# Dilated attention and gated unit: eight transfer semaphores in the scheduler's model, the v block moved to partitions 16 to 127, w_out exchanged on TensorE

## The chip, the cores and the metric

The kernel runs on one core of a Trainium2 chip. The time is that of one execution on the device in microseconds (us), taken as the median of several runs. The core has a matmul engine (TensorE, PE in the profile), a vector engine (VectorE, DVE), an engine for activations and copies (ScalarE, ACT), GpSimd (POOL), and a queue from which transfers are issued in order (SyncE, SP). The transfers themselves run on 16 transfer engines. On-chip data lies in 128 partitions of SBUF[...].

## The reference: what is computed

```python
# q, k, v: (8, 8, 576, 64)  batch, heads, positions, head size; float32
scores = q @ k.transpose(0, 1, 3, 2) / 8
rel = pos[:, None] - pos[None, :]
mask_plain = (rel >= 0) & (rel < 32)                       # heads 0 to 3
mask_dil = (rel >= 0) & (rel < 128) & (rel % 4 == 0)       # heads 4 to 7
attn = softmax(where(mask, scores, -1e9)) @ v
x = attn.transpose(0, 2, 1, 3).reshape(8, 576, 512)
# gated unit, per batch
gate = sigmoid(causal_conv(x, conv_w))                     # 5 taps, per channel
out = (gate * (x @ w_val)) @ w_out                         # (8, 576, 512) float32
```

A batch is handled as two units of four heads: one dilated, one plain. In a dilated unit the positions are sorted by their remainder modulo 4, so that the dilated window becomes a plain band of 32 in each of the four sets of 144 positions.

## The kernel before

The kernel is fully unrolled. Every piece of work is a task with the engines it may run on, its cost there, what it depends on, and a key. A greedy scheduler, at build time, runs through a model of the engines, takes again and again the task that can start first (among those that can start about then, the one with the lowest key), and emits all instructions in the order of the modelled start times. Each engine executes its own instructions in that order. So the keys and the modelled costs change the order of the work, and in part the engine, but not what is computed.

```python
KEY = {"L": 2.5, "cv": -28.5, "T": -2.0, "ET": -28.0, "S": -10.2, "X": -30.2, "M": -1.7,
       "A": -17.7, "N": -14.4, "XT": 3.7, "XE": -24.0, "C": 1.1, "H": -26.4, "V": 4.1,
       "G": -9.6, "O": 12.5, "P": -23.7, "SP": 2, "W": 5.4, "WV": 1, "WO": 2}
# L loads, T transposes of q and k, ET their eviction, S scores, X exp, M mask, A attention,
# N division, XT transposes of x, XE their eviction, C conv, H tanh, V x @ w_val, G gate,
# O output product, P its eviction; W: penalty for a change of TensorE's configuration;
# WV, WO: the unit behind whose loads w_val and w_out are loaded
...
    def start_of(self, t, eng):
        s = self.free_at[eng]
        if eng == "PE" and t.cfg != self.cfg and self.cfg is not None:
            s += self.SWITCH
        for d in t.deps:
            s = max(s, d.fin + self.LAT)
        if t.after:                      # a load does not start before the load ahead of it
            s = max(s, t.after.start)
        ...
        return max(s, self.slot_for(t)[0])
...
    # in commit(): a transfer in the model
        if t.load:
            self.dma = max(self.dma, s + 1.4) + t.load
            t.fin = self.dma + 0.6
...
    def fill(self, a, b):                # matmuls on a zero tile where TensorE would be idle (line 604)
        ...
```

The tasks of the loads, with the modelled transfer time as the last number, and the layout of the dilated v. `rows` is v as (positions of a set, head, 4 x 64 values): the first block has the positions 0 to 79 of each set, the second the positions 32 to 143, both from partition 0 on.

```python
    KB = (80, 112)
    T1 = TT - KB[1]          # TT = 144
...
    def load_vd(u, n, z):
        b = units[u][0]
        rows = v[b, 4:8].rearrange("h (p r) d -> p h (r d)", r=R)
        nc.sync.dma_start(out=vas[z][n % 2], in_=rows[z * T1:z * T1 + KB[z]])
...
            L[u] = dma(f"ld{name}{u}", j0 + KEY["L"], 1.8, ...)               # q or k: 576 KB
            ldv[u] = [dma(f"vd{z}{u}", j0 + KEY["L"], (1.0, 1.4)[z], ...)     # dilated v: 320, 448 KB
            ldv[u] = [dma(f"vp{u}{h}", j0 + KEY["L"], 1.4, ...)               # plain v: 384 KB, twice
...
        if u == KEY['WV']:
            load_w("val", moe_w_val, w_val[0], 0)      # two loads of 512 KB, casts to bf16
            exchanged_val()
        if u == KEY['WO']:
            load_w("out", moe_w_out, w_out[0], 6)
            exchanged_out()
```

The conv leaves its result for the second half of the positions with the two halves of the partitions exchanged. So a second copy of w_out is needed, with its rows exchanged in the same way; it is made by two transfers from SBUF to SBUF (line 644):

```python
    def exchanged_out():
        for h in range(2):
            W_OX.append(dma(f"out_x{h}", 11, 0.9, lambda h=h: nc.sync.dma_start(
                out=w_out[1][64 * h:64 * h + 64], in_=w_out[0][64 - 64 * h:128 - 64 * h]),
                W_OK["out"]))
```

The lines that the prediction speaks of: 370 and 373 load q and k (dilated and plain), 380 the dilated v, 388 and 392 the plain v, 591 issues the stores, 604 is the idle fill, 447 the exp, 427 the scores, 561 the product with w_val, 577 the one with w_out, 582 its eviction, 281 and 279 are the copies and casts through a helper.

Of the kernel before, what the change touches and what calls it, by code (L numbers as in the profile page):

```python
# [13 lines left out]
def hi_bf16(ap: bass.AP) -> bass.AP:  # L14
# [2 lines left out]
    return b[idx]  # L17


KEY = {"L": 2.5, "cv": -28.5, "T": -2.0, "ET": -28.0, "S": -10.2, "X": -30.2, "M": -1.7,  # L20
       "A": -17.7, "N": -14.4, "XT": 3.7, "XE": -24.0, "C": 1.1, "H": -26.4, "V": 4.1,
       "G": -9.6, "O": 12.5, "P": -23.7, "SP": 2, "W": 5.4, "WV": 1, "WO": 2}


class Task:
# [16 lines left out]
class Plan:  # L42


    LAT = 0.09
    SWITCH = 0.095
    BIAS = {"DVE": 0.4, "POOL": -0.8}
    GAP = 0.35
# [3 lines left out]
    def __init__(self, pairs, score_pairs):  # L52
        self.tasks = []
        self.free_at = {e: 0.0 for e in self.SLACK}
        self.banks = [0.0] * (2 * pairs)
        self.score_pairs = score_pairs
        self.scores = []
        self.cfg = None
        self.dma = 0.0
        self.port = {"DVE": 0.0, "POOL": 0.0}  # L60
        self.idle = None
        self.done = []
# [22 lines left out]
# [6 lines that stand above are left out]
        if t.after:  # L91
            s = max(s, t.after.start)
        if eng in t.port:
            s = max(s, self.port["POOL" if eng == "DVE" else "DVE"])
        return max(s, self.slot_for(t)[0])

    def fits(self, t, eng):
        if len(t.opts) == 1:
# [4 lines left out]
    def commit(self, t, eng, s):  # L103
        inf = float("inf")
        occ, lat = t.opts[eng]
        before = self.free_at[eng]
        self.free_at[eng] = s + occ
        t.fin = s + lat
        if t.load:
            self.dma = max(self.dma, s + 1.4) + t.load  # L110
            t.fin = self.dma + 0.6
        if eng in t.port:
            self.port[eng] = s + lat
        if eng == "PE":
            self.cfg = t.cfg
            self.fill(before, s)
        if t.need:
            t.slot = self.slot_for(t)[1]
            for n in t.slot:
                self.banks[n] = inf  # L120
            if t.need == "score":
                self.scores.append(inf)
                t.order = len(self.scores) - 1
            t.last = 0.0
        for f in t.frees:
            f.holders -= 1
            f.last = max(f.last, t.fin + self.LAT)
            if f.holders == 0:
                for n in f.slot:
                    self.banks[n] = f.last  # L130
                if f.need == "score":
                    self.scores[f.order] = f.last
        t.start, t.eng = s, eng
        self.done.append(t)
# [52 lines left out]
def kernel(  # L187
# [17 lines left out]
    W = 32  # L205
    TT = S // R
    QB = TT // 2
    KB = (80, 112)
    T1 = TT - KB[1]
    JP, JD = 9, 18  # L210
    scale = 1.0 / float(D) ** 0.5
    NCH = Dm // 128
# [36 lines left out]
    gy = consts.tile([128, NCH, 2, B, HALF], BF16, name="gy")  # L249

    ident_b = consts.tile([128, 128], BF16, name="ident_b")
    ident_2 = consts.tile([128, D], BF16, name="ident_2")
    ident_f = consts.tile([8, 8], FP32, name="ident_f")
    mask_d = consts.tile([128, HALF], BF16, name="mask_d")
# [42 lines left out]
    def const(name, eng, dur, emit, deps=(), key=-50):  # L297
        return plan.add(name, key, {eng: (dur, dur + 0.05)}, lambda t: emit(), deps,
                        port=("POOL",))

    c_warm = const("warm0", "DVE", 0.5, lambda: nc.vector.memset(warm, 0.0), key=-60)  # L301
    c_eye = const("eye", "POOL", 1.0, lambda: eye(ident_b, 128), key=-60)

    def dil_mask():
        nc.gpsimd.memset(mask_d, 1.0)
        for z in range(2):
            band(mask_d[:, 2 * QB * z:2 * QB * (z + 1)].rearrange("p (h t) -> p h t", h=2),
                 z * (QB - T1), [[0, 2], [1, QB]], 1)

# [27 lines left out]
    def dve_consts():  # L337
        for x in kTs:
            nc.vector.memset(x[:, 0:W], 0.0)
            nc.vector.memset(x[:, W + 2 * S:], 0.0)  # L340
        for x in ets:
            nc.vector.memset(x[:, :, HALF:], 1.0)
        nc.vector.memset(xT[:, :, :, 0:K - 1], 0.0)
        nc.vector.memset(vps[0][0:W // 2, 0], 0.0)
    c_dv = const("dve_consts", "DVE", 2.2, dve_consts, key=-59)


# [29 lines left out]
    def load_vd(u, n, z):  # L377
        b = units[u][0]
        rows = v[b, 4:8].rearrange("h (p r) d -> p h (r d)", r=R)
        nc.sync.dma_start(out=vas[z][n % 2], in_=rows[z * T1:z * T1 + KB[z]])  # L380

    def load_vp(u, n, half):
        b = units[u][0]
# [235 lines left out]
    def load_w(name, src, dst, key):  # L619
        parts = []  # L620
        for half in range(2):
            deps = [W_OK["val"][2 * half], W_OK["val"][2 * half + 1]] if name == "out" else []
            ld = dma(f"w_{name}{half}", key, 1.7, lambda half=half: nc.sync.dma_start(  # L623
                out=wst[half],
                in_=src.rearrange("(c p) n -> p c n", p=128)[:, 2 * half:2 * half + 2]), deps, lane=lane)
            for c in range(2):
                parts.append(add(
                    f"cast_{name}{half}{c}", key + 2, {"ACT": (0.52, 0.62), "DVE": (0.35, 0.42)},
                    lambda t, half=half, c=c: copy(t, dst[:, 2 * half + c], wst[half][:, c]),
                    [ld], port=("DVE",)))  # L630
        W_OK[name] = parts
# [9 lines left out]

    def exchanged_out():
        for h in range(2):
            W_OX.append(dma(f"out_x{h}", 11, 0.9, lambda h=h: nc.sync.dma_start(
                out=w_out[1][64 * h:64 * h + 64], in_=w_out[0][64 - 64 * h:128 - 64 * h]),
                W_OK["out"]))

    ldq, ldk, ldv, cvq, cvk = {}, {}, {}, {}, {}
    Tq, Tk, Eq, Ek = {}, {}, {}, {}
# [6 lines left out]
    for u in range(NU):  # L656
# [4 lines left out]
        for name, L, TQ in (("q", ldq, Tq), ("k", ldk, Tk)):  # L661
            dep = []
            if u >= NQ:
                p = u - NQ
                if units[p][1]:
                    dep = [TQ[p]]
                else:
                    dep = [(cvq if name == "q" else cvk)[p]]
            L[u] = dma(f"ld{name}{u}", j0 + KEY["L"], 1.8, lambda u=u, name=name: load_q(u, name), dep, lane=lane)
        if d:  # L670
            dep = [cvv[(same[-2], e, z)] for e in range(2) for z in range(2)] if len(same) > 1 else []
            ldv[u] = [dma(f"vd{z}{u}", j0 + KEY["L"], (1.0, 1.4)[z],
                          lambda u=u, n=len(same), z=z: load_vd(u, n, z), dep, lane=lane)
                      for z in range(2)]
        else:
            dep = [cvp[2 * same[-2] + e] for e in range(2)] if len(same) > 1 else [c_dv]
            ldv[u] = [dma(f"vp{u}{h}", j0 + KEY["L"], 1.4,
                          lambda u=u, n=len(same), h=h: load_vp(u, n, h), dep, lane=lane)
                      for h in range(2)]
            for name, C, L, TQ, cs in (("k", cvk, ldk, Tk, kcs), ("q", cvq, ldq, Tq, qcs)):  # L680
                dep = [TQ[same[-2]]] if len(same) > 1 else []
                C[u] = add(f"cv{name}{u}", j0 + KEY["cv"], {"POOL": (1.10, 1.16), "ACT": (1.05, 1.15)},
                           lambda t, u=u, name=name: copy(
                               t, (qcs if name == "q" else kcs)[(u // 2) % 2].rearrange(
                                   "p j h d -> p h j d"),
                               (qns if name == "q" else kns)[u % NQ].rearrange(
                                   "p (h j d) -> p h j d", h=2, j=JP)),
                           [L[u]] + dep, port=("POOL",))
# [120 lines left out]
    for n in range(NF):  # L809
        for f in range(2):  # L810
            z = len(ST)
            b0, b1 = 128 * n // HALF, (128 * n + 127) // HALF
            key = 8 * b1 + 7 + KEY["O"] + (z % 4)
            ou = add(f"O{f}{n}", key, {"PE": (0.86, 1.03)}, lambda t, f=f, n=n: outs(t, f, n),
                     [GA[(b, c)] for b in range(b0, b1 + 1) for c in range(NCH)]
                     + (W_OX if f else W_OK["out"]), cfg="F", need="bank")
            cp = add(f"P{f}{n}", 8 * b1 + 7 + KEY["P"], {"ACT": (0.52, 0.60), "DVE": (0.60, 0.68)},
                     lambda t, ou=ou, f=f, n=n, z=z: out_copy(t, ou, f, n, z),
                     [ou] + ([ST[z - NO]] if z >= NO else []), frees=[ou])
            ST.append(dma(f"st{f}{n}", key - 20, 0.7, lambda f=f, n=n, z=z: store(f, n, z), [cp]))  # L820

    plan.run()

# [29 lines left out]
```

## Time and profile before

| | |
|---|---|
| time, median of 3 runs | 202.44 us (201.51 to 207.02) |
| span of the profiled execution | 200.5 us |
| TensorE busy, matmuls | 168.8 us (84%), 2887 of them |
| VectorE busy | 122.1 us (61%) |
| ScalarE busy | 122.7 us (61%) |
| GpSimd busy | 60.0 us (30%) |
| transferred | 43.94 MB, of them 33.56 MB read from memory and 9.44 MB written to it |
| packets of the main queue | 81.2% of the 16 engines' span |
| granted TensorE clock, mean | 0.961 of full speed |

The busy times are for the whole span and don't say when an engine is the limit; the slices, the stages and the issue queue, which the prediction shows, do. TensorE's busy time includes the idle fill: 14.3 us in 51 matmuls (line 604), all of it in the first 50 us. The exchange of w_out shows as two transfers of 256 KB with 10.7 us from issue to landing.

### The profile page before, as it was taken

The numbers are of one execution on the slowest core, as the hardware profiler recorded it, in microseconds if no ns is written. First come the engines' busy times: TensorE is split into PE (matmuls) and PEld (weight loads), VectorE is DVE, ScalarE is ACT, GpSimd is POOL, SyncE is SP. The second block draws the span as 40 slices with busy tenths as digits, with TensorE's granted clock in tenths as the row PEclk, the third lists the DMA queues.
The fourth block names the chain that finished last, engine by engine and source line by source line (L and its number), as shares of the span: only waits on it lengthen the run. The fifth ranks groups of instructions, "written<-read, shape, count | busy, mean of one in ns | idle before, by whom it ended". The sixth has DMA issues, their size and how long they took to land.

```text
span 200.5 us, 6725 instructions
## 1 busy us (share of the span) xinstructions
PE 168.8 (84%) x2887; PEld 115.0 (57%) x2887; DVE 122.1 (61%) x233; ACT 122.7 (61%) x205; POOL 60.0 (30%) x98
## 2 busy tenths in 40 slices
PE   7987799695999788769889697999899979989890
PEld 2544476473576646646466474767567767557640
DVE  4393759575377767437656483776767877861600
ACT  2555857572884848812878357957778588465242
POOL 7964041334430543525352320833161000000000
PEclk9999979998899999957999999999999999999998
DMA  6999999999999999979699979996872001133156
GB/s 214 277 257 309 306 316 259 233 241 261 243 264 219 253 332 280 281 221 293 196 296 247 275 257 305 294 246 220 284 233 111 3 0 56 56 105 128 32 143 224
DMA packets 32262, 43.94 MB, mean 219 GB/s; under 512 B 1909, under 2 KB 20325, under 8 KB 32234
## 3 DMA queue, kind: packets, MB, share of 16 engines
q1 hardware_dynamic: 32224, 43.52, 81.2%
q8 instruction: 22, 0.36, 0.8%
q14 instruction: 6, 0.05, 0.1%
q10 hardware_dynamic: 10, 0.01, 0.0%
HBM read 33.56 MB, written 9.44 MB: 214 GB/s over the span
## 4 chain that ended last, share of the span: by engine, by line
PE 50%; DMA 16%; SPq 9%; ACT 9%; issue 7%; DVE 6%; ACTq 0%; DVEq 0%
DMA kn<-in_k_dram 16%; PE ps L577 15%; PE ps L561 13%; PE ps L546 8%; PE ps L408 3%; ACT osb L582 3%; PE ps L427 3%; SPq L623 3%; SPq L392 3%; SPq L370 3%; PE ps L491 2%; PE ps L464 2%; ACT et L447 2%; DVE qT L281 2%; PE ps L512 1%
## 5 line engine op out<-in xcount | busy, mean ns | idle before, releaser
L447 ACT ACTIVATE et<-ps 128x576 bf16<-128x576 f32 x64 | 41.0, 655 | 15.1 <-PE ps L427 15.0
L577 PE MATMUL ps<-w_out,gy 128*128 128x512 bf16 x144 | 38.0, 398 | 4.3 <-ACT osb L582 2.8
L561 PE MATMUL ps<-xT,w_val 128*128 128x288 bf16 x256 | 37.6, 296 | 2.0 <-issue 2.0
L582 ACT ACTIVATE osb<-ps 128x512 f32<-128x512 f32 x35 | 20.6, 602 | 26.3 <-PE ps L577 20.2
L281 POOL CAST vd<-va 80x512 bf16<-80x512 f32 (+1 forms) x32 | 21.3, 691 | 47.0 <-DMA va<-in_v_dram 37.2
L570 DVE SCALAR_TENSOR_TENSOR gy<-gy,ps 128x576 bf16<-128x576 bf16 x32 | 24.1, 752 | 11.5 <-PE ps L561 11.0
L561 PEld LDWEIGHTS <-w_val 128*128 128x128 bf16 x256 | 24.0, 101 | 10.1 <-issue 3.2
L546 PE MATMUL ps<-xT,diag 64*64 64x288 bf16 x640 | 24.4, 289 | 1.8 <-ACT qT L279 0.6
L577 PEld LDWEIGHTS <-gy 128*128 128x128 bf16 x144 | 13.6, 101 | 18.1 <-issue 6.6
L279 ACT COPY qT<-ps 128x576 bf16<-128x576 bf16 x24 | 14.8, 647 | 13.6 <-PE ps L408 12.3
L474 DVE TENSOR_TENSOR xnd<-ps,rec 72x512 bf16<-72x512 f32 x32 | 22.0, 687 | 1.1
L453 DVE TENSOR_TENSOR et<-et,mask_d 128x576 bf16<-128x576 bf16 x32 | 19.1, 605 | 5.3 <-ACT et L447 5.1
L546 PEld LDWEIGHTS <-diag 64*64 64x64 bf16 x640 | 18.2, 108 | 5.0 <-issue 3.9
L427 PE MATMUL ps<-qT,kT 64*64 64x96 bf16 (+1 forms) x640 | 19.7, 206 | 1.1 <-DVE kT L281 0.5
L554 ACT ACTIVATE gy<-ps 128x576 bf16<-128x576 f32 x32 | 20.2, 658 | 0.4
L453 DVE TENSOR_TENSOR et<-et,mask_p 128x576 bf16<-128x576 bf16 x32 | 16.0, 505 | 6.7 <-ACT et L447 6.1
L281 POOL CAST vpb<-vp 128x768 bf16<-128x768 f32 x16 | 13.0, 837 | 21.8 <-DMA vp<-in_v_dram 9.8
L427 PEld LDWEIGHTS <-kT 64*64 64x64 bf16 (+1 forms) x640 | 12.8, 103 | 11.5 <-issue 7.2
L279 ACT COPY kT<-ps 128x576 bf16<-128x576 bf16 x22 | 13.6, 646 | 9.4 <-PE ps L408 7.5
L279 ACT COPY xT<-ps 128x576 bf16<-128x576 bf16 (+1 forms) x19 | 15.6, 823 | 4.2 <-PE ps L577 2.8
L604 PE MATMUL ps<-warm 128*128 128x512 bf16 x51 | 14.3, 411 | 2.0 <-DVE warm L301 1.3
L503 DVE TENSOR_TENSOR xnp<-ps,den 96x768 bf16<-96x768 f32 x16 | 15.3, 954 | 0.5
(63 smaller groups left out, 172.9 us busy)
## 6 DMA issues: line engine op xcount, KB each, us to landing
qn<-in_q_dram SPq DMA_DIRECT2D x16, 576.0 KB, 11.1
kn<-in_k_dram SPq DMA_DIRECT2D x16, 576.0 KB, 12.2
out_dram<-osb SPq DMA_DIRECT2D x24, 256.0 KB, 4.1
vp<-in_v_dram SPq DMA_DIRECT2D x15, 384.0 KB, 14.2
va<-in_v_dram SPq DMA_DIRECT2D x8, 448.0 KB, 11.0
va<-in_v_dram SPq DMA_DIRECT2D x8, 320.0 KB, 10.2
out_dram<-osb SPq DMA_DIRECT2D x8, 192.0 KB, 3.9
wst<-in_moe_w_val_dram SPq DMA_DIRECT2D x2, 512.0 KB, 11.9
```

The lines of the kernel that those rows point to most:

```text
L279: nc.scalar.copy(out=dst, in_=src)
L281: op(t.eng).tensor_copy(dst, src)
L427: nc.tensor.matmul(out=ps[po:po + pn, x, out_c:out_c + ln], lhsT=kw[rb, k0:k0 + (pn - 1) * kstep + 1:kstep], rhs=qT[rb, q0:q0 + (ln - 1) * ...
L447: nc.scalar.activation(out=ets[(2 * i + hf) % NE][:, :, 0:HALF], in_=ps[:, :, 0:HALF], func=AF.Exp, scale=scale)
L453: op(t.eng).tensor_tensor(out=ev, in0=ev, in1=m.to_broadcast([128, 2, HALF]), op=ALU.mult)
L474: nc.vector.tensor_tensor(out=xnd[i % 2][:, 4 * hf:4 * hf + 4].rearrange("p (x j) h d -> p x (j h) d", x=2), in0=av[:, :, :, 0:D], in1=rec ...
L546: nc.tensor.matmul(out=ps[o:o + 64, 512 * f:512 * f + HALF], lhsT=diag[lo:lo + 64, c * K + kk, :], rhs=xT[lo:lo + 64, b % NX, c, f * HALF ...
L554: nc.scalar.activation(out=gy[:, c, :, b, :], in_=ps[:, :, 0:HALF], func=AF.Tanh, scale=0.5)
L561: nc.tensor.matmul(out=ps[:, 512 * f:512 * f + HALF], lhsT=w_val[f][:, mc, c * 128:(c + 1) * 128], rhs=xT[:, b % NX, mc, K - 1 + f * HALF: ...
L570: nc.vector.scalar_tensor_tensor(out=y, in0=y, scalar=1.0, in1=ps[:, :, 0:HALF], op0=ALU.add, op1=ALU.mult)
L577: nc.tensor.matmul(out=ps, lhsT=y[:, c, 128 * n:128 * n + 128], rhs=w_out[f][:, c, :], start=(c == 0), stop=(c == NCH - 1))
L582: nc.scalar.activation(out=osb[z % NO], in_=bank(ou), func=AF.Copy, scale=0.5)
```

## The change

There are three parts. First, the scheduler's model learns that at most eight transfers are under way (`LANES`): a transfer can't start before the one eight places ahead of it has landed. With this come new transfer times, from measured packet rates, a new set of keys, and both weights one unit earlier in the order of loads. Second, the second block of the dilated v goes to the partitions 16 to 127; partitions 0 to 15 of its two buffers are zeroed once, and casts, masks and the attention matmul of this block work on 128 rows. Third, the copy of w_out with exchanged halves is made by four matmuls with an exchanged identity, and by two evictions, in place of the two transfers. The purpose is that the emitted order fits the arrival of the data, that the transfers have less to do, and that the loads spread over the partitions.

```diff
-KEY = {"L": 2.5, "cv": -28.5, "T": -2.0, "ET": -28.0, "S": -10.2, "X": -30.2, "M": -1.7,
-       "A": -17.7, "N": -14.4, "XT": 3.7, "XE": -24.0, "C": 1.1, "H": -26.4, "V": 4.1,
-       "G": -9.6, "O": 12.5, "P": -23.7, "SP": 2, "W": 5.4, "WV": 1, "WO": 2}
+KEY = {"L": 107.8, "cv": -124.6, "T": -1.8, "ET": -73.4, "S": -44.5, "X": -131.1, "M": -134.6, "A": -61.1,
+       "N": -69.6, "XT": -4.5, "XE": -25.9, "C": -13.0, "H": -17.0, "V": 4.2, "G": -107.0, "O":
+       16.7, "P": -80.5, "SP": 2, "W": 23.7, "WV": 0, "WO": 1}
...
+    LANES = 8
...
-        return max(s, self.slot_for(t)[0])
+        s = max(s, self.slot_for(t)[0])
+        if t.load:
+            while True:
+                n = sum(1 for a, _ in self.lanes if a <= s)
+                if n < self.LANES or self.lanes[n - self.LANES][1] <= s:
+                    break
+                s = self.lanes[n - self.LANES][1]
+        return s
...
             t.fin = self.dma + 0.6
+            self.lanes = sorted(self.lanes + [(s, t.fin)])
...
-    KB = (80, 112)
+    KB = (80, 128)
     T1 = TT - KB[1]
+    Z1 = 16
...
+    swap_b = consts.tile([128, 128], BF16, name="swap_b")
...
+        for h in range(2):
+            nc.vector.tensor_copy(swap_b[:, 64 * h:64 * h + 64], ident_b[:, 64 - 64 * h:128 - 64 * h])
...
+        for x in vas[1]:
+            nc.vector.memset(x[0:Z1], 0.0)
...
-        nc.sync.dma_start(out=vas[z][n % 2], in_=rows[z * T1:z * T1 + KB[z]])
+        if z == 0:
+            nc.sync.dma_start(out=vas[z][n % 2], in_=rows[0:KB[0]])
+        else:
+            nc.sync.dma_start(out=vas[z][n % 2][Z1:KB[1]], in_=rows[T1 + Z1:TT])
...
-            W_OX.append(dma(f"out_x{h}", 11, 0.9, lambda h=h: nc.sync.dma_start(
-                out=w_out[1][64 * h:64 * h + 64], in_=w_out[0][64 - 64 * h:128 - 64 * h]),
-                W_OK["out"]))
+            def swap(t, h=h):
+                for c in range(2):
+                    nc.tensor.matmul(out=pair(t)[:, 512 * c:512 * c + 512], lhsT=swap_b,
+                                     rhs=w_out[0][:, 2 * h + c, :], start=True, stop=True)
+            x = add(f"out_s{h}", 10, {"PE": (0.43, 0.60)}, swap,
+                    W_OK["out"] + [c_sw], cfg="F", need="pair")
+            W_OX.append(add(
+                f"out_x{h}", 11, {"ACT": (0.95, 1.05), "DVE": (1.16, 1.24)},
+                lambda t, x=x, h=h: copy(
+                    t, w_out[1][:, 2 * h:2 * h + 2, :].rearrange("p c n -> p (c n)"), pair(x)),
+                [x], frees=[x]))
...
-    weights, each half: 1.7        # the modelled transfer times; the lines are shortened to them
+    weights, each half: 1.6
-    q or k: 1.8
+    q or k: 1.75 if d else 1.85
-    dilated v: (1.0, 1.4)[z]
+    dilated v: (1.25, 1.75)[z]
-    plain v, each half: 1.4
+    plain v, each half: 2.0
-    store: 0.7
+    store: 0.8
```

## The prediction

> **What bounds the kernel now.** I read the page's 40 slices first, to see whether one limit holds all the time.
>
> ```profile
> PE   7987799695999788769889697999899979989890
> DMA  6999999999999999979699979996872001133156
> GB/s 214 277 257 309 306 316 259 233 241 261 243 264 219 253 332 280 281 221 293 196 296 247 275 257 305 294 246 220 284 233 111 3 0 56 56 105 128 32 143 224
> ```
>
> A slice is 5 us. Two limits follow each other. Up to about 150 us the transfer engines are full (9s) and TensorE has holes (6s to 8s). After that the inputs are all in, the transfers carry only stores, and TensorE is at 9. The stage table puts figures on it: all work first, then the idle-fill matmuls alone (line 604, on a zero tile, which produce nothing); the first numbers after the stretch's length are TensorE's busy time.
>
> ```profile
> 0.00:50.00 50.00, 39.73 (x622) 25.30 (x623) 31.33 (x66) 28.17 (x47) 22.42 (x54) 0.95 1.04 267
> 50.00:150.00 100.00, 85.86 (x1546) 59.94 (x1545) 63.71 (x120) 65.99 (x110) 36.74 (x43) 0.96 0.99 263
> 150.00:200.50 50.50, 43.19 (x723) 29.74 (x721) 27.03 (x49) 28.49 (x49) 0.83 (x1) 0.98 0.26 85
> ...
> 0.00:50.00 50.00, 14.33 (x51) 4.67 (x51) 0.95 1.04 267
> ```
>
> Useful TensorE time is 168.8 - 14.3 = 154.5 us. What the span has beyond it, 200.5 - 154.5 = 46.0 us, is lost as follows: 50 - (39.7 - 14.3) = 24.6 in the first 50 us, 14.1 in the next 100, 7.3 at the end. No other engine is near: VectorE 122, ScalarE 123 of 200.5. So the change is worth what it takes from these 46 us, and the last 7.3 hold little.
>
> Third I read the issue queue (SPq) in order of time, since every load and store leaves through it in one order.
>
> ```profile
> 40.38 5.91 SPq L392 DMA_DIRECT2D vp<-in_v_dram  x2
> 46.39 4.69 SPq L644 DMA_DIRECT2D w_out<-w_out  x2
> 51.17 0.54 SPq L370 DMA_DIRECT2D qn<-in_q_dram  x1
> ...
> 107.44 9.38 SPq L591 DMA_DIRECT2D out_dram<-osb  x7
> 117.42 1.14 SPq L373 DMA_DIRECT2D qn<-in_q_dram  x1
> ```
>
> An unhindered issue takes 0.3 to 0.5 us; here two take 5.91, and a load can stand behind seven stores for 10 us. Two limits work on this queue. Following the transfers' completion semaphores through the trace, I count eight in rotation, and a transfer waits for the landing of the one eight places ahead: the four issues at 55.88, 57.10, 58.54 and 59.59 each come 0.06 to 0.24 us after such a landing. And single issues last up to 5.1 us by themselves, with all semaphores free[...]. The kernel's scheduler knows neither: it lets a load start as soon as its buffer is free, and so orders its tasks for arrivals that don't happen. The waits that follow:
>
> ```profile
> POOL vd L281 <- DMA va<-in_v_dram: 37.2, 11, 7.7
> ACT osb L582 <- PE ps L577: 20.2, 18, 4.7
> ACT et L447 <- PE ps L427: 15.0, 16, 3.1
> POOL kc L281 <- DMA kn<-in_k_dram: 13.8, 7, 3.3
> ```
>
> The casts that wait for transfers show that data comes late, though GpSimd itself (60 us busy) is not the limit.
>
> [...] here 224 elements took 245 ns, 0.91 per ns[...].
>
> **The change, part by part.**
>
> *w_out exchange.* It removes two transfers of 256 KB. At 263 GB/s, 0.52 MB hold the full transfer engines for 2.0 us, and the issue queue for 4.69. It adds four matmuls of 512 columns: the output projection's median is 379 ns recorded, but four in a row end after 0.88 us in the chain, so 0.9 us of TensorE. Two evictions of 1024 columns are added. ScalarE took 602 ns for 512 columns and 655 for 576, so 0.83 ns a column: an estimate of 1.03 us each; 2.1 us on an engine that has 77 us free. Net on the path: -2.0 of transfer time while transfers bind, +0.9 of TensorE. As the product's first use was near 48 us, against w_out being cast at 31.8 us, latency isn't the point. I count -1.0.
>
> *Second v block at partitions 16 to 127.* The same 448 KB, the same 1 KB rows, 112 partitions. [...] its packets are only 6.3 of 43.9 MB, so I count 0 to -0.5. The zeroed rows add two memsets of 16 x 1024 fp32: by 0.91 elements per ns 1.1 us each, on VectorE in the first 5 us. VectorE ended its constants at 2.98 us and had nothing until 6.34, so 0. The cast and the matmul work on 128 rows instead of 112: the 80-row matmul took 195 ns and the 112-row one 193, so rows cost nothing.
>
> *Weights one unit earlier.* Each weight is 1.05 MB, 4.0 us of transfers. In the new order units 1 and 2 come 4.0 us later, unit 3 not. The value weights were first used at 32.35 us and had landed at 21.6, so their earlier arrival buys nothing by itself. Units 1 and 2 had waited some us for TensorE after landing. I count +1.
>
> *Scheduler and keys.* The new rates are near what the packets took: a 576 KB load's packets fill 16 engines for some 2.0 us (1.8 assumed before), the two 1 KB-row v blocks 1.4 and 2.0 (1.0 and 1.4 before), the two 512 B-row v blocks 2.1 each (1.4 before). The old estimate is thus some 15% short of a batch's loads, and had no limit of eight. With both, tasks stand in the order in which data really comes, and a late task no longer holds the in-order engines. New keys also rank masks and gates first on VectorE and keep TensorE longer in one configuration (5.4 to 23.7). [...] Where this pays is the middle: 14.1 us lost, 11.0 of it outside of one stall of 3.1 us near 84 us, in which all engines stood and which I can't assign to order. I take a little under half of the 11.0, 5 us, one of the first 24.6 (arrivals set most of these), and 1 of 7.3; these three are choices.
>
> Sum: -1.0 + 0 + 1 - 5 - 1 - 1 = -7 us. 202.4 - 7 = 195.4 us.
>
> **Rivals.** (1) *Transfers bind anyway.* Until 150 us they were full; the same bytes less 0.5 MB remain, so a better order can't bring the last input much before 147, and the 43 us of TensorE work after it stay: 200 to 202. For it: the row of 9s. Against: 39.7 MB (50 us at 267, 100 at 263 GB/s) moved in those 150 us, 33.6 of them read from memory and 0.5 the exchange, so some 5.6 MB were stores, which could go later; and how much work is left at that point is a matter of order. (2) *The keys are fitted to a model, not to the chip.* Units 1 and 2 arrive 4 us later in the stretch that is already starved, conv is put 13 ahead of other work, and TensorE may wait for its own preference: 203 to 208. For it: keys of hundreds look like a search. Against: the model is nearer to the trace than before. (3) *Model now right, search good*: the first 50 us, too, are filled, since about 5 of 16 units had landed by then while only 25 of 154 us of work were done; half of the 24.6 and half of the 14.1 go, 183 to 186. Against: the waits there are a chain through all engines with few units in flight, and order can't lengthen the supply.
>
> **Range and chances.** My 195.4 lies between rivals 1 and 3. Rivals 1 and 2 end the range above, 3 below: 186 to 204. 2% faster is under 198.4; I give it 0.63, since several independent terms point that way; within 2%, 0.25 (rival 1, or a smaller gain); slower than 206.5, 0.12 (rival 2).
>
> **What would show it.** Right: no w_out from the issue queue, and two wide evictions of it; useful TensorE time near 155.4; TensorE over 88 of 100 us between 50 and 150; the issue queue without 5 us issues; fill time not above 14.3; the last input landing at 145 or earlier. Wrong: the last input still near 148 and over 43 us of TensorE after it (rival 1); useful work in the first 50 us under 25.4 (weights too early, rival 2); or over 35 (rival 3). A stall of some us without releaser, as near 84, at another place would blur it by 3 us either way.

## The result and the profile after

The changed kernel takes 194.51 us (median of 4 runs, 192.27 to 196.18), the kernel before beside it 203.13 (4 runs). The ratio is 0.952, 95% interval 0.937 to 0.966: clearly faster, and near the 195.4 that I had predicted. (The ratios here leave disturbed executions out, so a median can differ from what its ratio says.)

The slices of the page after, 4.8 us each: TensorE, its granted clock, the transfer engines, and what they moved.

```profile
PE   7999988788888779989896998989999989999890
PEclk9999999999999999999999699999999999999998
DMA  5999999999999999999999839996451312035256
GB/s 199 269 384 235 379 255 288 234 264 278 232 341 335 252 290 233 366 294 303 296 210 269 245 115 259 361 246 247 169 172 52 113 58 110 3 104 160 68 169 215
```

The shape is that of before: transfers full, then stores only. But TensorE has fewer holes, its clock is below 9 in one slice instead of five (the last slice aside), and the transfer engines drop to 3 near 112 us and are no longer full from 129 us on, although the last loads are issued at 140 us: late in the loads they wait for the kernel. The stages after, all work first, then the idle fill alone (now line 627):

```profile
0.00:50.00 50.00, 43.88 (x689) 27.12 (x690) 35.26 (x73) 31.78 (x53) 25.50 (x56) 1.00 1.04 275
50.00:150.00 100.00, 87.47 (x1715) 62.93 (x1714) 73.31 (x132) 69.19 (x114) 36.18 (x43) 0.98 0.92 254
150.00:191.40 41.40, 34.90 (x491) 23.17 (x489) 19.87 (x36) 22.04 (x37) 0.00 (x0) 0.99 0.32 103
...
0.00:50.00 50.00, 15.34 (x51) 4.77 (x51) 1.00 1.04 275
50.00:150.00 100.00, 0.39 (x1) 0.10 (x1) 0.98 0.92 254
```

Useful TensorE time is 166.25 - 15.72 = 150.5 us; before it was 154.5. Lost are 50 - 43.88 + 15.34 = 21.5 us in the first stage (24.6 before), 12.9 in the second (14.1) and 6.5 in the third (7.3). So the 9.1 us by which the span fell, from 200.5 to 191.4, are 3.1 + 1.2 + 0.8 of idle time and 4.0 of shorter work. The last part I had not predicted at all. The costliest groups show it: the same matmuls, before and then after (the mean of one in ns stands behind the busy time).

```profile
L577 PE MATMUL ps<-w_out,gy 128*128 128x512 bf16 x144 | 38.0, 398 | 4.3 <-ACT osb L582 2.8
L561 PE MATMUL ps<-xT,w_val 128*128 128x288 bf16 x256 | 37.6, 296 | 2.0 <-issue 2.0
```

```profile
L600 PE MATMUL ps<-w_out,gy 128*128 128x512 bf16 x144 | 35.7, 380 | 2.9 <-ACT osb L605 1.9
L584 PE MATMUL ps<-xT,w_val 128*128 128x288 bf16 x256 | 36.0, 286 | 3.5 <-issue 2.2
```

398 fell to 380 ns and 296 to 286, with nothing changed in them. What differs is the granted clock. The page of before:

```profile
PEclk9999979998899999957999999999999999999998
```

Stages of before, TensorE only (length, busy time and matmuls, then the clock): each of its three stretches at half clock, with the 3.4 us ahead of it.

```profile
20.90:24.30 3.40, 1.97 (x43) 1.00 1.07 298
24.30:27.80 3.50, 3.50 (x88) 0.52 1.09 266
44.90:48.30 3.40, 0.96 (x18) 1.00 1.04 289
48.30:51.70 3.40, 3.40 (x13) 0.51 1.20 215
82.50:85.90 3.40, 1.27 (x44) 1.00 1.13 232
85.90:92.70 6.80, 5.80 (x39) 0.50 0.84 260
```

And the one stretch of after, with the same time ahead of it, all engines:

```profile
101.40:104.80 3.40, 1.75 (x26) 0.99 (x25) 3.16 (x5) 1.81 (x4) 1.11 (x1) 1.00 1.06 298
104.80:108.30 3.50, 3.50 (x71) 2.87 (x73) 1.23 (x4) 1.78 (x3) 1.13 (x2) 0.51 0.87 236
```

Each time TensorE had stood still for 1.4 to 2.4 of the 3.4 us before; then it ran at half clock for 3.4 us or twice that. The matmuls took nearly twice as long there: in the chain of before, eight with w_out took 3.39 us from 48.44 on, 424 ns each, and twenty at full clock 4.49 us from 190.47 on, 224 ns each. So I estimate that half of the busy time of such a stretch is due to the clock: before (3.50 + 3.40 + 5.80) / 2 = 6.3 us, after 3.50 / 2 = 1.7. The difference of 4.6, less the 1.2 us of the four new matmuls, is 3.4 of the 4.0 us by which useful time fell. So in TensorE's own account these holes came with a second cost beside their length, by this estimate some 1.7 us for each 3.4 us at half clock.

That the span falls by the same amount is not shown. This account compares one execution of each kernel, and the mean clock differs between executions of one kernel: 0.940 to 0.982 for the kernel before, 0.969 to 0.990 for the changed one. And a run described below, with the exchange back on the transfers, has three stretches at half clock, 10.2 us in all:

```profile
PEclk9999999997978999999987999999999999999999
```

Its span is 192.4 us, only 1.0 us more than that of the changed kernel with its 3.4 us. The other way round, five executions of the run with the limit of eight alone had a mean clock of 0.989 to 0.998 and still took 199.4 to 201.8 us. So the gain does not hang on the clock alone.

The issue queue after, some of its issues in order of time:

```profile
3.17 1.25 SPq L646 DMA_DIRECT2D wst<-in_moe_w_val_dram  x2
37.96 5.22 SPq L415 DMA_DIRECT2D vp<-in_v_dram  x2
103.06 4.01 SPq L614 DMA_DIRECT2D out_dram<-osb  x4
107.16 0.54 SPq L393 DMA_DIRECT2D qn<-in_q_dram  x1
140.04 0.42 SPq L401 DMA_DIRECT2D va<-in_v_dram  x1
140.52 0.50 SPq L403 DMA_DIRECT2D va<-in_v_dram  x1
```

The value weights now come right after the first unit. No transfer of w_out is left. The single issues of several us are still there (37.96: 5.22 us for two), which the new model doesn't know either. Stores still stand ahead of loads (103.06), and the last v block leaves at 140.52 and lands at 145.2, against 147.9 before. Its cast starts at 145.6 without a wait. GpSimd's lengthiest waits after (total us, times, longest),

```profile
POOL vpb L294 <- DMA vp<-in_v_dram: 21.7, 8, 5.0
POOL vpb L294 <- PE ps L514: 16.9, 3, 12.5
POOL vd L294 <- DMA va<-in_v_dram: 14.2, 6, 7.2
```

have 14.2 us for dilated v instead of 37.2, but 21.7 for plain v (9.8 before), and more time in which GpSimd waits for TensorE to have read a buffer that it is to fill (16.9 for plain v, 5.1 before).

### The profile page after: what moved, and what is told of

It reads as the page before. It is cut to its first block, busy times and chain, and to the rows that moved or that the text cites. A ratio compares the mean times of both kernels' runs of the same rounds, so it can differ in the third digit from the quotient of the medians.

```text
span 191.4 us, 6733 instructions
## 1 busy us (share of the span) xinstructions
PE 166.2 (87%) x2892; PEld 113.2 (59%) x2892; DVE 128.4 (67%) x239; ACT 123.0 (64%) x204; POOL 61.7 (32%) x99
## 4 chain that ended last, share of the span: by engine, by line
PE 57%; DVE 12%; ACT 11%; DMA 9%; issue 6%; POOL 1%; ACTq 0%; SPq 0%; DVEq 0%
PE ps L600 14%; PE ps L584 13%; DMA kn<-in_k_dram 8%; PE ps L569 7%; PE ps L627 6%; PE ps L431 5%; PE ps L450 4%; ACT et L470 4%; PE ps L487 3%; ACT osb L605 3%; DVE et L476 3%; PE ps L514 2%; PE ps L535 2%; DVE qT L294 2%; ACT qT L292 2%
## 5 line engine op out<-in xcount | busy, mean ns | idle before, releaser
L470 ACT ACTIVATE et<-ps 128x576 bf16<-128x576 f32 x64 | 40.6, 653 | 17.4 <-PE ps L450 17.2
L584 PE MATMUL ps<-xT,w_val 128*128 128x288 bf16 x256 | 36.0, 286 | 3.5 <-issue 2.2
L600 PE MATMUL ps<-w_out,gy 128*128 128x512 bf16 x144 | 35.7, 380 | 2.9 <-ACT osb L605 1.9
L294 POOL CAST vd<-va 80x512 bf16<-80x512 f32 (+1 forms) x32 | 20.7, 678 | 33.1 <-DMA va<-in_v_dram 14.2
L569 PE MATMUL ps<-xT,diag 64*64 64x288 bf16 x640 | 25.1, 287 | 2.4 <-issue 0.7
L294 POOL CAST vpb<-vp 128x768 bf16<-128x768 f32 x16 | 13.5, 863 | 38.6 <-DMA vp<-in_v_dram 21.7
L476 DVE TENSOR_TENSOR et<-et,mask_p 128x576 bf16<-128x576 bf16 x32 | 18.7, 591 | 7.0 <-ACT et L470 6.3
L476 DVE TENSOR_TENSOR et<-et,mask_d 128x576 bf16<-128x576 bf16 x32 | 20.2, 636 | 4.3 <-ACT et L470 3.9
L600 PEld LDWEIGHTS <-gy 128*128 128x128 bf16 x144 | 12.7, 98 | 15.6 <-issue 3.1
L292 ACT COPY xT<-ps 128x576 bf16<-128x576 bf16 (+1 forms) x20 | 15.7, 786 | 7.2 <-PE ps L551 3.7
L292 ACT COPY qT<-ps 128x576 bf16<-128x576 bf16 x22 | 13.6, 643 | 10.5 <-PE ps L431 7.8
L450 PE MATMUL ps<-qT,kT 64*64 64x96 bf16 (+1 forms) x640 | 18.6, 203 | 1.6 <-ACT kT L292 1.0
L450 PEld LDWEIGHTS <-kT 64*64 64x64 bf16 (+1 forms) x640 | 12.4, 102 | 12.3 <-issue 8.1
L627 PE MATMUL ps<-warm 128*128 128x512 bf16 x52 | 15.7, 429 | 1.3 <-DVE warm L314 1.3
L292 ACT COPY kT<-ps 128x576 bf16<-128x576 bf16 x21 | 12.9, 644 | 4.6 <-PE ps L431 2.7
```

The source lines that it names most:

```text
L292: nc.scalar.copy(out=dst, in_=src)
L294: op(t.eng).tensor_copy(dst, src)
L450: nc.tensor.matmul(out=ps[po:po + pn, x, out_c:out_c + ln], lhsT=kw[rb, k0:k0 + (pn - 1) * kstep + 1:kstep], rhs=qT[rb, q0:q0 + (ln - 1) * ...
L470: nc.scalar.activation(out=ets[(2 * i + hf) % NE][:, :, 0:HALF], in_=ps[:, :, 0:HALF], func=AF.Exp, scale=scale)
L476: op(t.eng).tensor_tensor(out=ev, in0=ev, in1=m.to_broadcast([128, 2, HALF]), op=ALU.mult)
L569: nc.tensor.matmul(out=ps[o:o + 64, 512 * f:512 * f + HALF], lhsT=diag[lo:lo + 64, c * K + kk, :], rhs=xT[lo:lo + 64, b % NX, c, f * HALF ...
```

## The experiments

All have the kernel before beside them on the same chip. **Theory A**: the order of the work brings the gain, through the better model (A1) or through keys fitted to it (A2). **Theory B**: the two other parts relieve the transfers. As a greedy schedule jumps at small changes, some of the runs keep the order of everything else exactly. Four runs (the v block back, the two halves of the model, the model alone) have the same 23 executions of the kernel before beside them, with a median of 206.57 us (199.79 to 212.48); their ratios rest on the two shortest of these, so where it matters the quotient of the medians is given as well.

### The parts without the schedule

```diff
-KEY = {"L": 107.8, ...}          # the keys of before again, all of them
+KEY = {"L": 2.5, ...}
-    LANES = 8
+    LANES = 1000
-    the new transfer times (1.6; 1.75 if d else 1.85; (1.25, 1.75)[z]; 2.0; 0.8)
+    the old ones           (1.7; 1.8;                 (1.0, 1.4)[z];   1.4; 0.7)
```

> The changed kernel with the old keys, the old transfer times and no limit of eight in the scheduler: only the v block at partitions 16 to 127 and the exchange of w_out on TensorE are new. Theory A (the order of the work brings the gain): within 2 us of before, 200 to 204. Theory B (the transfers are relieved by the two parts): most of the gain is here, 194 to 197.

Measured: 206.83 us, ratio 1.016 (1.008 to 1.023), above the range of theory A and far from that of theory B. Theory B falls: without the schedule, the exchange on TensorE and the v placement are a little worse than nothing.

### The exchange back on the transfers, order kept

```diff
             def swap(t, h=h):
-                for c in range(2):
-                    nc.tensor.matmul(out=pair(t)[:, 512 * c:512 * c + 512], lhsT=swap_b, ...)
+                pass
 ...
-                lambda t, x=x, h=h: copy(t, w_out[1][:, 2 * h:2 * h + 2, :]..., pair(x)),
+                lambda t, x=x, h=h: nc.sync.dma_start(
+                    out=w_out[1][64 * h:64 * h + 64], in_=w_out[0][64 - 64 * h:128 - 64 * h]),
```

> The changed kernel in the very same order of all other work, but the second w_out is made by the two transfers again, issued where its evictions stood; the four matmuls are left out. By my prediction's term of 1.0 us: 194 to 197. If the exchange relieves the transfers more than that (theory B): 197 to 200.

Measured: 197.08 us, just above the first range and at the foot of the second, ratio 0.959 (0.950 to 0.969), against 0.952 (0.937 to 0.966) for the changed kernel. The ratios are 0.008 or 1.6 us apart, but their intervals overlap: a direct effect near my 1.0 us is possible, a large one is not. What the exchange costs in the changed kernel (busy time or duration in ns behind the operation):

```profile
L669 PE MATMUL ps<-w_out,swap_b x4: 379/379/379, 24.7 to 25.9; 128*128 128x512 bf16 x4
L292 ACT CAST w_out<-ps x2: 1012/1015/1018, 25.4 to 27.6; 128x1024 bf16<-128x1024 f32 x2
```

Four matmuls of 379 ns and two evictions of 1.015 us, which I had estimated at 1.03.

### The second v block back at partition 0, order kept

```diff
-    KB = (80, 128)
+    KB = (80, 112)
-        if z == 0:
-            nc.sync.dma_start(out=vas[z][n % 2], in_=rows[0:KB[0]])
-        else:
-            nc.sync.dma_start(out=vas[z][n % 2][Z1:KB[1]], in_=rows[T1 + Z1:TT])
+        nc.sync.dma_start(out=vas[z][n % 2], in_=rows[z * T1:z * T1 + KB[z]])
-        for x in vas[1]:
-            nc.vector.memset(x[0:Z1], 0.0)
```

> The changed kernel in the very same order, the second dilated v block again on partitions 0 to 111, with no zeroed rows. By my prediction (no effect of the placement): 193 to 196, no difference that can be measured from the changed kernel. [...]

Measured: 191.24 us, ratio 0.950 (0.933 to 0.967), against 0.952. The time is below the range, and the placement makes no difference that can be measured. This is the lowest median of the study, but by its ratio it does not beat the changed kernel.

### Model and keys apart

First the changed kernel with the keys of before and nothing else.

> The changed kernel with the old keys alone (weights again behind units 1 and 2). Theory A1 (the better model of the transfers is what orders the work better): most of the gain stays, 195 to 198. Theory A2 (model and keys belong together, the keys were fitted to this model): most of the gain is lost, 200 to 205. Theory B: 194 to 197, as the parts stay.

Measured: 193.65 us, ratio 0.955 (0.947 to 0.962): the whole gain, a little below the ranges of A1 and B, with the old keys and with the weights behind units 1 and 2 as before. A2 falls, and so does what I had said of the keys' new ranks on top of the model. Then the reverse: the new keys, with `LANES = 1000` and the old transfer times.

> The changed kernel with the old transfer times and no limit of eight, new keys kept. Theory A1: the gain is lost, 200 to 204. Theory A2: lost as well, 199 to 206. If the keys' new ranks alone (masks and gates first, TensorE longer in one configuration) bring it: 193 to 197. Theory B: 194 to 197.

Measured: 198.57 us, ratio 0.975 (0.968 to 0.982). It lies in none of the four ranges. Alone the keys bring about half. The two are not a sum: each is a way to a better order.

### The model in two halves

Both with the parts and the old keys; one has the limit of eight with the old transfer times, the other the new times with `LANES = 1000`.

> The changed kernel with the old keys and the old transfer times, the limit of eight kept. If the limit of eight is what the old order lacked: 193 to 197. If the transfer times are: 200 to 207.

> The changed kernel with the old keys and the new transfer times, without the limit of eight. If the transfer times are what the old order lacked: 193 to 197. If the limit of eight is: 200 to 207. If either one alone gives half: about 199 in both runs.

Measured: 1.000 (0.992 to 1.008) for the limit alone and 1.017 (1.002 to 1.032) for the times alone. By these ratios neither half brings anything, both together 0.955. By the medians (201.82 and 204.31 us against 206.57) they are 0.977 and 0.989, so a smaller gain of the limit alone is not excluded. Each run lands where it was expected if the other half were the cause, so neither is the cause of the whole gain by itself.

### The model alone, on the kernel before

```diff
+    LANES = 8
 ...  the limit in start_of() and commit(), and the new transfer times, as in the change
      keys of before, w_out exchanged by transfers, v block from partition 0
```

> The kernel before with nothing but the scheduler's model changed: the limit of eight and the new transfer times. Old keys, w_out exchanged by transfers, v block from partition 0. Theory A1 (the model is the cause, as the run with the new model and the old keys says): 192 to 197. If the model only pays together with the exchange on TensorE and the v block: 199 to 204.

Measured: 204.33 us, ratio 1.018 (1.001 to 1.035), by the medians 0.989. So the model does not bring the gain by itself. From the run with the new model and the old keys this one differs by the place of v, which made no difference above and is in no cost of the model, and by the exchange, whose direct cost above was about 1.6 us; yet here are 6 percent, or 4 by the medians. By elimination the exchange acts through the order that is planned with it; it was not taken back with this order kept. The stages of both, this kernel first (all work, then the idle fill in the first stage):

```profile
0.00:50.00 50.00, 40.87 (x622) 24.67 (x626) 26.66 (x63) 27.57 (x45) 24.11 (x55) 0.95 1.03 276
50.00:150.00 100.00, 87.29 (x1585) 61.41 (x1578) 67.86 (x119) 65.99 (x112) 32.45 (x39) 0.97 0.92 251
150.00:202.10 52.10, 44.43 (x704) 29.88 (x703) 26.37 (x49) 30.39 (x51) 3.06 (x5) 1.00 0.30 97
...
0.00:50.00 50.00, 18.32 (x66) 6.06 (x66) 0.95 1.03 276
```

```profile
0.00:50.00 50.00, 42.87 (x680) 26.99 (x686) 34.12 (x74) 29.75 (x49) 24.09 (x55) 1.00 1.04 271
50.00:150.00 100.00, 89.48 (x1697) 65.27 (x1710) 68.15 (x132) 70.22 (x119) 36.81 (x44) 0.98 0.93 261
150.00:191.40 41.40, 34.64 (x508) 23.70 (x510) 21.53 (x38) 21.05 (x36) 0.00 (x0) 1.00 0.28 90
...
0.00:50.00 50.00, 17.32 (x59) 5.97 (x64) 1.00 1.04 271
```

By 50 us TensorE has done 40.87 - 18.32 = 22.6 us of useful work here, 42.87 - 17.32 = 25.6 there, and after 150 us 44.4 are left against 34.6. The issue queue of this kernel shows one possible way to such a delay (some of its issues):

```profile
73.02 0.61 SPq L402 DMA_DIRECT2D vp<-in_v_dram  x1
80.55 3.10 SPq L601 DMA_DIRECT2D out_dram<-osb  x5
83.70 0.62 SPq L402 DMA_DIRECT2D vp<-in_v_dram  x1
94.75 0.41 SPq L383 DMA_DIRECT2D kn<-in_k_dram  x1
100.86 3.02 SPq L601 DMA_DIRECT2D out_dram<-osb  x4
103.98 0.65 SPq L402 DMA_DIRECT2D vp<-in_v_dram  x1
```

Between the two halves of a plain v block five stores stand, the first of which the queue can only issue at 80.55, 7 us after the half before them; at 100.86 four stores again stand ahead of a v half. The cast waits for v:

```profile
POOL vpb L291 <- DMA vp<-in_v_dram: 33.0, 8, 12.1
```

But loads stand behind stores in the fast kernels too. In the run with the new model and the old keys four stores are issued at 75.93, ahead of a k load at 80.49 and a v half at 81.52, and the queue's total wait for evictions is nearly as long in the changed kernel as here (the changed kernel first):

```profile
SPq L614 <- ACT osb L605: 67.5, 24, 6.5
SPq L601 <- ACT osb L592: 75.5, 25, 6.4
```

In the kernel before it is 40.6 us, in the run with the new model and the old keys 50.5. So this wait does not follow the time of the kernel. Nor does GpSimd's wait for q, k and v together: 76.5 us here, 75.8 in the run with the new model and the old keys.

### Is it one lucky order?

Each key times a random factor within 2 percent, drawn once, for the changed kernel and for the one just shown.

> The changed kernel with each key scaled by a random factor within 2 percent, drawn once. If the better model makes good orders as such: 192 to 197. If the new kernel is one lucky order that the search of keys found: 197 to 205.

Measured: 195.42 us (192.21 to 199.74), with the kernel before at 205.43 beside it, 0.951 by the medians.

> The kernel before with the new model (204.3 measured) and each old key scaled by a random factor within 2 percent, drawn once. If that order was an unlucky one: 194 to 200. If the exchange by transfers spoils every order: 202 to 206.

Measured: 204.92 us, ratio 1.001 (0.995 to 1.007). Both neighbours stay where their originals are. So the gain is no single lucky order, and the lack of it no single unlucky one; but 2 percent is a small neighbourhood.

### Stores from another queue

To test whether loads behind stores are what makes the order without gain slow, the stores were issued from ScalarE's queue, all orders kept, in that kernel and in the changed one.

```diff
-            nc.sync.dma_start(out=out[b, f * HALF + c:f * HALF + c + ln, :],
+            nc.scalar.dma_start(out=out[b, f * HALF + c:f * HALF + c + ln, :],
```

> The kernel before with the new model (204.3 measured), every order kept, but the stores issued from ScalarE's queue in place of the common one, so that no load stands behind a store. Theory Q (this order is slow because loads stand behind stores that wait for their evictions): 195 to 200 in spite of the issues' cost on ScalarE. Theory R (the order of the compute work itself is what differs): 203 to 208.

> The same with the changed kernel: every order kept, stores from ScalarE's queue. Theory Q as a limit of the changed kernel too: 188 to 192, and the last load lands before 140. If TensorE and buffers bind it, not the issue queue: 194 to 198, as ScalarE has 48 issues more.

Measured: 219.86 us, ratio 1.070 (1.053 to 1.087), and 204.1 us, ratio 0.986 (0.981 to 0.992). Both lie above all of their ranges. Against the common queue these are 5.1 and 3.6 percent more (1.070 / 1.018 and 0.986 / 0.952). ScalarE in the first of the two, in order of time (in brackets its idle time, and what ended it):

```profile
87.01 0.60 ACT L592 ACTIVATE osb<-ps 128x512 f32<-128x512 f32 x1 [2.24 <-DMA out_dram<-osb]
90.96 2.27 ACTq L601 DMA_DIRECT2D out_dram<-osb  x2
93.33 0.65 ACT L457 ACTIVATE et<-ps 128x576 bf16<-128x576 f32 x1 [5.73 <-DMA vp<-in_v_dram]
```

At 93.33 an exp, which works on scores alone, starts after 5.73 us of idle time that ended with the landing of a v load. It stood behind the two stores at 90.96, and those waited for semaphores that two v loads, eight places ahead of them, still had: these landed at 90.88 and 92.89, and the stores were issued at 90.96 and 92.91. The eight are shared by both queues here (in the kernel before, too, the conv load that ScalarE's queue issues at 0.81 us uses one of them), so the wait came along to ScalarE and stopped its computing. The test therefore says nothing for or against the loads behind stores; it shows what such a wait did in a queue that also computes.

## Why the prediction was right, and where it was not

**The sum** was right: 195.4 predicted, 194.51 measured, and the range held. Its working was right only in part, and some of the agreement is luck.

**"I take a little under half of the 11.0, 5 us, one of the first 24.6 ... and 1 of 7.3."** This step was mis-sized in two of its three terms. The middle gave 1.2 us instead of 5, the first 50 us 3.1 instead of 1 (there I had also put 1 us against the change, for the weights), the end 0.8. Together 5.1 of 9.1 us of the span. All this is for one pair of executions.

**A term that is missing is the clock.** The prediction counts idle time only. It speaks of a stall of all engines near 84 us that it can't assign (ScalarE and GpSimd in fact worked 0.91 and 1.36 of the 3.3 us from 83.7 on), but not of the half clock that follows. The changed kernel had one stretch at half clock instead of three, and useful time fell by 4.0 us where I expected it to rise by 0.9 to 155.4. In this account the right total came from two errors that cancel, which is luck. How much of the 4.0 us other executions would show is open: with three stretches at half clock the run with the exchange put back is only 1.0 us longer in span.

**Exchange: "-1.0".** Not contradicted: 1.6 us with the order kept, within the intervals.

**v block: "0".** Right. The 0.5 us that I allowed beside it was my estimate, with no trace behind it. The two memsets were recorded at 0.91 us each and started 1.07 us apart (I said 1.1, from 245 ns for each of six memsets of 224 elements in the kernel before), on a VectorE that then still idled until 7.07.

**Weights: "+1".** Not tested by itself. With the old places and keys the time is the same.

**Scheduler and keys.** That they, not the direct cost of the parts, carry the change was right; that the model with the old keys would pay only in a plan with the exchange on TensorE was not foreseen. The 15 percent by which I called the old transfer times short were reckoned too low: four loads of q and k and the v blocks of a batch are 12.4 us by the old times, and 15.6 by the packet times that I named, so 20 percent. And I added the model and the keys as if each gave some of the gain. The runs show no sum:

| parts | limit of eight | transfer times | keys | ratio to before |
|---|---|---|---|---|
| new | - | - | old | 1.016 |
| new | new | - | old | 1.000 |
| new | - | new | old | 1.017 |
| new | new | new | old | 0.955 |
| new | - | - | new | 0.975 |
| new | new | new | new | 0.952 |
| old | new | new | old | 1.018 |

**The rivals.** Rival 1 said that the last input can't land much before 147 and that the 43 us of work behind it stay. The first half was nearly right, 145.2; the second was wrong: at 150 us 34.9 us were left, as 4.3 us more of useful time was done by then and the total was 4.0 smaller. Rival 2 (keys fitted to the model, not to the chip) has a true core: on top of the new model the new keys bring nothing that can be measured, 0.952 against 0.955. Rival 3 didn't come: by 50 us 28.5 us of useful work were done, not 35.

**What I had said would show it.** No w_out in the queue and two wide evictions: yes. TensorE over 88 of 100 us in the middle: 87.5, just missed; the last input at 145 or earlier: 145.2, just missed. Useful work near 155.4: 150.5, missed. No issues of 5 us, fill not above 14.3: missed (5.22 for two, 15.7). These last two were not needed for the gain.

**What stays open** is why the place of the exchange in the plan decides whether the better model pays. Without it on TensorE, single casts wait longer for v (12.1 us against 4.2 at most with the new model and the old keys), and loads stand behind stores; but loads do so in the fast kernels too. That this is the cause, and not a companion of another compute order, is not shown, since the run that was to tell was slowed for a reason of its own. Whether the new keys would rescue the model without the exchange on TensorE was not tried either.

## What to carry to other kernels

Look at the granted clock in the slices before you divide the lost time, and do not take the division of one pair of executions for the cause: here matmuls at half clock made up much of it, yet a run with three such stretches was nearly as fast. A better model in a greedy scheduler need not be a gain by itself: here each half of it alone brought little or none, so test the order on the chip with the pieces apart and with jittered keys before one of them is given the credit. Before you move issues to the queue of an engine that computes, look at what they wait for: here ScalarE stood for 5.73 us because of loads from another queue.

## What the runs showed of the hardware that I had not expected

TensorE went to half clock after standing still for as little as 1.4 us within 3.4 us (20.9 to 24.3 us before). It stayed there for 3.4 us twice and for 6.8 us once before, and for 3.4 us after (the end of the span aside). Yet it stood still for 2.23 us after 65.8 us in the changed kernel without any drop in the clock. So the length of the hole alone does not decide, and what does is not shown. A wait for one of the eight transfer semaphores stopped ScalarE just as it stopped the common queue, whose issues came 0.06 to 0.24 us after such landings in the kernel before. ScalarE stood for 5.73 us, until a v load landed that ScalarE never reads. And single issues took 5.11 and 5.51 us in the issue queue itself, at 59.59 and 81.74 us in the kernel before, with their semaphores free since 59.36 and 81.30.
